# One filter spectrum of a block convolution by a direct transform instead of two stages with shuffles, on one core of Trainium2

## The chip, the cores and the metric

The kernel runs on one core of a Trainium2 chip, as one launch. The metric is the device time of one execution in microseconds (us), the median of several runs. The engines are TensorE (PE, with its weight loads PEld), VectorE (DVE), ScalarE (ACT), GpSimd (POOL) and SyncE (SP), which here only issues DMAs. Every engine runs its own instructions in the order in which the program has them, so an instruction that waits holds up all that stand behind it on its engine.

## What is computed

The reference, cut to what matters (S = 2048 tokens, D = 640 columns, F = 1728, bf16):

```
x  = A_q
q  = layernorm(x)
ks = sum over t<4 of k shifted by t tokens * shift_k          # four taps
kv = ks * v
y  = irfft(rfft(kv, padded to 2S) * rfft(ssm_k, padded to 2S))[:S] + kv * ssm_D
h  = x + q * y                                                # a causal convolution along S, per column
n  = layernorm(h)
out = h + (silu(n @ w_gate) * (n @ w_up)) @ w_down            # the FFN
```

## The kernel before, in words

The tokens are cut into four blocks j = 0 to 3 of 512, the columns into two halves c = 0, 1 of 320. For each block and half the kernel computes a spectrum X of kv and a spectrum K of the filter ssm_k (1024 points, the block padded with as many zeros), multiplies spectra of blocks whose indices add up to j, and transforms back. The convolution of a block is followed by its layernorm and its FFN. A token 4p+b of a block lies in partition p, at place b.

**Two ways to a spectrum.** Block 0 goes the dense way (`dense_c`, L692): for each of four groups h of frequencies, `dense_h` (L678) multiplies the four slices b by 128x128 tables for the real and the imaginary part. These are 8 matmuls of 320 columns (op `df`), accumulated in PSUM and moved to SBUF by one instruction of 640 columns (`de`). Blocks 1 to 3 go in two stages (`conv_c`, L1086). `fwd` (L648) multiplies each slice b by two tables (op `s1`, 2 matmuls of 128x128 by 320 columns), moves the result to SBUF (`e1`, 640 columns) and then, by four DMAs from SBUF to SBUF of 160 KB (`sh`, one for each group, each needing all four `e1`), brings every fourth partition together. `spec` (L730) multiplies a shuffled group by a small table (op `s2`, 4 matmuls of 128x64 tables by 320 columns, pairs of which run beside each other on the two halves of the array) and moves the spectrum to SBUF (`e2`). The way back has the same two stages (`i2`, `e3`, shuffles `rs`, `i1`); in block 0 it is dense (`di`).

A name such as `s1K10b2` is read: first stage, filter K (or values X), block 1, column half 0, slice b2. `s2K10h1` is the second stage of group h1. The name of `G` in `shK10G1` is the group. Further ops in what follows: `kvn`, `kva`, `kvv` (DVE: taps, products and sums that make kv), `tap` (moves the taps from PSUM to SBUF), `m1`, `m2`, `cr`, `ci`, `ac` (DVE: products and sums of spectra), `kf` (DVE: the filter spectrum of a block put together with that of the block before), `w` and `h` (ACT and DVE: the convolution's result, scaled and added to x), `bn`, `ag`, `va`, `nr`, `nm` (layernorm statistics; `nr` is a power on POOL), `hn` (the normalised row, on ACT or DVE), `tr` (10 transposes on PE; L1119), `te` (their move to SBUF on ACT), `gu` (FFN, gate or up), `si` (silu, ACT), `gm` (gate times up, DVE), `dn` (FFN, down), `l0s`, `l0v` (sums for the first layernorm, ACT).

**Data.** Filters of blocks 1 to 3 come from DRAM by a transposing DMA (`kraw`, L597) and four copies of 80 KB (`shk`), which bring them into the layout of 4p+b; a first stage or a dense transform needs all four. The inputs k, v and x come as `kin`, `vin` and `x`; `kin` and `vin` of blocks after the first share one buffer each, so that a load waits until the one before has been used. The dense tables `den` (8 DMAs of 256 KB; ("f",h) forward, ("i",h) back) lie where w_down (`wd`) is put later, so `load_weights` (L1130) lets `wd` wait for the last op that reads a dense table (`den_last`). The tables of the two stages (`tab`, 640 KB, L1261) come in one DMA: 256 columns of first stage, 256 of last stage back (s1i), 1024 of second stage (w2s) and 1024 of its inverse (w2i) (a column is 2 bytes in each of 128 partitions, so 256 bytes).

**Warm-up.** `warm` (WARM = 5 and 4 matmuls of 512 columns) and five `fill` ops (2 such matmuls each) compute nothing that is used; they stand in PE's order like other work.

**The order.** It is not found at run time. `_PLAN` (L1288) is a packed table that gives every op its engine, its place in that engine's order, its buffer, and for some DMAs one more op to wait for (written `a<b`: a is issued when b is done). `plan` (L101) reads it, `emit` (L151) writes the instructions and the semaphore waits. All matmuls are recorded under the helper's line L515, evacuations under L495 (ACT) and L496 (DVE), DVE two-operand ops under L737, DMA issues under L503.

Of the kernel before, what the change touches and what calls it, by code (L numbers as in the profile page):

```python
# [255 lines left out]
def _tables(R, neg=False):  # L256
# [27 lines left out]
    cols = [s1f.reshape(128, -1), s1i.reshape(128, -1), w2s, w2i.reshape(128, -1)]  # L284
# [33 lines left out]
def bass_sequential_preLN__ssm_conv_h3__swiglu_ffn__prompt_kernel(  # L318
# [21 lines left out]
    FILL = [2, 2, 2, 2, 2]  # L340
# [6 lines left out]
    ACCD = 2560  # L347
    KDMA = [[False, False], [True, True], [True, True], [True, True]]
# [5 lines left out]
    tab_np, (oS1, oS1I, oW2, oW2I, *more_) = _tables(R, PEC)  # L354
# [8 lines left out]
    with ExitStack() as es:  # L363
# [208 lines left out]
        def load_kv(j, c, prio):  # L572
# [12 lines left out]
            if j == 0:  # L585
                dma([(lambda: V2(kt, 3 * CW, CW, 4, CW), lambda: dram(K2, c * CW, [[R * D, 128], [D, 4], [1, CW]]))], 328, [], [(kt, 0)], prio,
                    name=f"kin{j}{c}o", eng=LE)
            else:
                dma([rows(0, 128)], 573, [], [(kt, 0)], prio, name=f"kin{j}{c}", eng=LE)
# [100 lines left out]
        nks = {}  # L690

        def dense_c(c):  # L692
# [10 lines left out]
            for h in range(R):  # L703
# [17 lines left out]
        den_last = [None]  # L721
# [8 lines left out]
        def spec(nm, r, u, h, dst, off, prio):  # L730
            pt = Pair("p2")
# [64 lines left out]
        def inv2(j, c, ht_, parts, prio):  # L796
# [12 lines left out]
            pe(all_, CW, len(all_) // 2, rd + [(TAB, 1)], [(pt, "*") for pt in pts], prio, reserve=[(ht_[h], 0) for h, _, _ in parts],  # L809
# [28 lines left out]
        def agm(l, j):  # L838
            o = oAG + j * 8
# [6 lines left out]
        def ln_stats(l, j, b, c, xt, prio):  # L846
            vec(dve1(CW, False), lambda v: v.bn_stats(st6(l, j, b, c), V(xt, b * D + c * CW, CW)), [(xt, (b, c))],  # L847
                [(ST, ("s", l, j, b, c))], prio, name=f"bn{l}{j}{b}{c}")

        def ln_aggr(l, j, b, prio):  # L850
            vec(0.16, lambda v: v.bn_aggr(ag(l, j, b), st6b(l, j, b)), [(ST, ("s", l, j, b, c)) for c in range(2)],
# [34 lines left out]
        def ln_act(l, j, prio):  # L886

            xt = xts[j]
            for b in range(4):
# [37 lines left out]
        def kv_block(j, c, prio):  # L927
# [10 lines left out]
            tm = [P.tile(f"t{j}{c}{i}", "PP") for i in range(3 if j else 4)]  # L938
            t0 = tm[0]

            def mul2(jj, a_, b_):
# [4 lines left out]
                def both():  # L946
# [3 lines left out]
                k0, st = ((3 - jj) * CW, -CW) if j else (3 * CW, 0)  # L950
                vec(dve2(2 * W4), tt(both, lambda: cyc(kt, k0, st), lambda: cyc(TAPS, jj * D + c * CW, D), ALU.mult),
                    [(kt, 0), (TAPS, (c, jj // 2))], [(a_, 0), (b_, 0)], prio, name=f"kvn{j}{c}")
# [5 lines left out]
            if j == 0:  # L958
# [101 lines left out]
        def conv_bp(j, c, bp, HTt, pr, ready=None):  # L1060
# [8 lines left out]
            if not ready:  # L1069
                pe(fns, CW, 4, [(HTt, h) for h in range(R)] + [(TAB, 0)], [(pt, "*")], pr, name=f"i1{j}{c}{bp}")  # L1070
# [15 lines left out]
        def conv_c(j, c):  # L1086
# [3 lines left out]
            uk = fwd(f"K{j}{c}", [(kts[j, c], oS1)], pb + 104)  # L1090
            ux = fwd(f"X{j}{c}", [(vins[j, c], oS1)], pb + 101)
# [38 lines left out]
        def load_weights():  # L1130
# [20 lines left out]
            piece([(lambda: V(WD, 13 * D, D, 0, 64), lambda: dram(B_w_down, 13 * 128 * D, [[D, 64], [1, D]]))], 82, [(WD, 13)], "wdl", [den_last[0]])  # L1151
# [93 lines left out]
        def block_j(j):  # L1245
# [5 lines left out]
            if j == 0:  # L1251
# [9 lines left out]
                dma([(lambda: tab[:, :], lambda: tab_dram.ap())], 900, [], [(TAB, 0), (TAB, 1)], 90, name="tab")  # L1261
# [116 lines left out]
```

## Time and profile before

| | us |
|---|---|
| median of 3 runs | 283.43 (282.67 to 283.63) |
| the profiled execution | 282.72 |
| its span, first to last instruction | 280.8 |
| PE busy in it | 270.0 |
| DVE busy | 229.0 |
| ACT busy | 198.2 |

The span is read from the profile, the execution's own time stands 1.9 us above it and 0.71 us below the median. Busy time of PE is that of instructions as modelled: a matmul counts from its start to its end, and matmuls overlap, so a busy PE can be slower than its peak. A row of the timeline is a run of like instructions: its start, its length, the engine, line, operation, shapes and count, and in brackets the idle time before it with what ended that.

### The profile page before, as it was taken

The page shows a single profiled execution, that of the slowest core. Times are in us where ns is not written, and L with a number is a line of the kernel's source. Part 1 is how long each engine was busy: PE and PEld are TensorE (multiplying, and loading weights), DVE is VectorE, ACT ScalarE, POOL GpSimd, SP SyncE. Part 2 cuts the span into 40 slices and gives each one's busy share as a digit, 9 for nine tenths or more (in the row PEclk, how much of TensorE's full clock was granted, in tenths as well). Part 3 has the DMA queues.
Part 4 walks back from the last instruction along what each step waited for, and adds up shares of the span by engine and source line. Part 5 has one row for each costly group of instructions (what it writes and reads, how often), then busy time and mean ns, then how long its engine had stood idle before and what let it go on. Part 6 is the DMA issues. An engine that isn't in the chain of part 4 may idle for free.

```text
span 280.8 us, 4821 instructions
## 1 busy us (share of the span) xinstructions
PE 270.0 (96%) x1735; PEld 149.8 (53%) x1735; DVE 229.0 (82%) x423; ACT 198.2 (71%) x322; POOL 13.9 (5%) x21
## 2 busy tenths in 40 slices
PE   8999996789999999999999999999999999999996
PEld 3667663355544467644344666544445675444574
DVE  3989999699999999999989999999997742224133
ACT  4648888799999979777899979769998830321100
POOL 1000100100000202000000103000002010000000
PEclk9999999799999999999999999999999999999999
DMA  6978979968986780685533364660012043000012
GB/s 189 267 234 259 213 234 247 261 167 249 307 262 208 231 260 7 167 229 177 175 103 98 97 232 137 168 237 1 0 70 99 21 77 89 0 2 0 0 37 82
DMA packets 54461, 41.37 MB, mean 147 GB/s; under 512 B 20195, under 2 KB 51748, under 8 KB 54438
## 3 DMA queue, kind: packets, MB, share of 16 engines
q1 hardware_dynamic: 54290, 41.02, 49.9%
q8 instruction: 14, 0.23, 0.3%
q14 instruction: 9, 0.07, 0.1%
q10 hardware_dynamic: 148, 0.04, 0.1%
HBM read 19.42 MB, written 2.62 MB: 78 GB/s over the span
## 4 chain that ended last, share of the span: by engine, by line
PE 63%; DVE 16%; DMA 8%; ACT 6%; SPq 4%; issue 2%; POOL 0%; ACTq 0%
PE ps L515 63%; DVE sb L737 15%; DMA sb<-in_A_k_dram 4%; SPq L503 3%; ACT sb L495 3%; DMA sb<-sb 3%; DMA sb<-cst_den 1%; ACT sb L1074 1%; SPq L597 1%; ACT sb L1173 1%; ACT L1173 0%; POOL stt L864 0%; DVE sb L1240 0%; ACT sb L879 0%; ACT sb L891 0%
## 5 line engine op out<-in xcount | busy, mean ns | idle before, releaser
L515 PE MATMUL ps<-sb 128*128 128x320 bf16 (+2 forms) x1259 | 226.8, 335 | 2.5 <-DVE sb L529 1.1
L737 DVE TENSOR_TENSOR sb<-sb 128x1280 bf16<-128x1280 bf16 (+5 forms) x264 | 174.3, 732 | 5.4 <-ACT sb L495 3.0
L515 PEld LDWEIGHTS ps<-sb 128*128 128x128 bf16 (+1 forms) x1259 | 120.3, 98 | 95.0 <-issue 7.8
L495 ACT ACTIVATE sb<-ps 128x640 bf16<-128x640 f32 (+2 forms) x161 | 113.3, 755 | 24.5 <-PE ps L515 18.4
L515 PE MATMUL ps<-sb,tab 128*64 128x320 bf16 (+2 forms) x432 | 53.0, 308 | 4.2 <-DMA sb<-sb 3.2
L1173 ACT ACTIVATE sb<-ps 128x1024 bf16<-128x1024 f32 (+2 forms) x32 | 29.1, 920 | 33.3 <-PE ps L515 33.2
L515 PEld LDWEIGHTS ps<-sb,tab 128*64 128x64 f16 (+2 forms) x432 | 26.2, 103 | 29.5 <-issue 10.3
L737 DVE TENSOR_TENSOR sb<-ps,sb 128x1024 bf16<-128x1024 f32 (+3 forms) x18 | 16.0, 893 | 26.2 <-PE ps L515 19.6
L864 POOL TENSOR_TENSOR stt<-stt 128x2 f32<-128x2 f32 (+1 forms) x12 | 12.9, 1080 | 213.7 <-DVE stt L863 183.8
L1074 ACT ACTIVATE sb<-ps,stt 128x320 f32<-128x320 f32 x32 | 17.8, 621 | 2.7 <-PE ps L515 2.3
L1078 DVE SCALAR_TENSOR_TENSOR sb<-sb,stt 128x320 bf16<-128x320 bf16 x32 | 16.7, 548 | 1.4 <-ACT sb L1074 1.4
L1240 DVE SCALAR_TENSOR_TENSOR sb<-ps,stt,sb 128x640 bf16<-128x640 f32 x12 | 10.6, 881 | 3.5 <-PE ps L515 3.4
L898 ACT ACTIVATE sb<-sb,stt 128x640 uint8<-128x640 bf16 x16 | 13.3, 831 | 0.1
L891 ACT ACTIVATE sb<-sb 128x640 uint8<-128x640 bf16 x16 | 11.9, 742 | 0.4 <-DMA sb<-in_A_q_dram 0.4
L916 ACT ACTIVATE sb<-sb,stt 128x640 uint8<-128x640 bf16 x12 | 9.9, 829 | 1.3 <-DVE stt L911 0.9
L1215 DVE SCALAR_TENSOR_TENSOR sb<-ps,stt,sb 128x320 bf16<-128x320 f32 x8 | 4.4, 551 | 6.7 <-PE ps L515 6.7
L879 ACT ACTIVATE sb<-sb,stt 128x640 bf16<-128x640 bf16 x7 | 6.4, 915 | 0.4 <-DVE stt L871 0.2
L878 DVE TENSOR_SCALAR sb<-sb,stt 128x640 bf16<-128x640 bf16 x9 | 3.9, 444 | 0.7 <-PE ps L1119 0.6
L847 DVE BATCH_NORM_STATS2 stt<-sb 128x6 f32<-128x320 bf16 x8 | 3.5, 482 | 0.0
L635 PE MATMUL ps<-sb 128*128 128x128 bf16 (+1 forms) x24 | 3.2, 225 | 0.1
L891 ACT ACTIVATION_READ_ACCUMULATOR sb<-sb 128x1 f32 x16 | 3.3, 204 | 0.0
L898 ACT ACTIVATION_READ_ACCUMULATOR sb<-sb,stt 128x1 f32 x16 | 3.2, 201 | 0.0
(26 smaller groups left out, 21.6 us busy)
## 6 DMA issues: line engine op xcount, KB each, us to landing
sb<-sb SPq DMA_DIRECT2D x72, 160.0 KB, 2.4
sb<-in_A_k_dram SPq DMA_DIRECT2D x6, 560.0 KB, 4.6
sb<-in_A_v_dram SPq DMA_DIRECT2D x8, 320.0 KB, 4.1
sb<-in_A_q_dram SPq DMA_DIRECT2D x8, 320.0 KB, 3.4
sb<-cst_den SPq DMA_DIRECT2D x8, 256.0 KB, 3.7
sb<-sb SPq DMA_DIRECT2D x24, 80.0 KB, 3.3
out_dram<-sb SPq DMA_DIRECT2D x12, 160.0 KB, 2.1
sb<-in_B_w_down_dram SPq DMA_DIRECT2D x3, 480.0 KB, 5.1
```

The lines of the kernel that those rows point to most:

```text
L495: fns = {"act": lambda a: a.activation(out=dst(), in_=src(), func=ACTF.Copy), "dve": lambda v: v.tensor_copy(out=dst(), in_=src())}
L503: fns = [(lambda g, d=d, s=s: g.dma_start(d(), s())) for d, s in subs]
L515: return lambda t: t.matmul(o(), l(), r(), start=st, stop=sp)
L737: return lambda v: v.tensor_tensor(out=o(), in0=a(), in1=b_(), op=op)
L864: P.op({"pool": 1.05}, lambda g: g.tensor_tensor(out=y, in0=va, in1=stt[:, oCO + 4:oCO + 4 + hi - lo], op=ALU.pow), c1 + [(ST, "half")], c ...
L891: P.op({"act": act_c(D) + 0.22}, lambda a, b=b, jt=jt: a.activation(out=JU(jt), in_=V(xt, b * D, D), func=ACTF.Copy, accum_out=tmv(l, j, 4 ...
L898: P.op({"act": act_c(D) + 0.3}, lambda a, b=b, jt=jt: a.activation(out=JU(jt), in_=V(xt, b * D, D), func=ACTF.Square, bias=tmv(l, j, 5)[:, ...
L916: P.op({"act": act_c(D) + 0.3}, lambda a, b=b, jt=jt: a.activation(out=JU(jt), in_=V(xt, b * D, D), func=ACTF.Square, bias=tmv(l, j, 5)[:, ...
L1074: P.op({"act": act_c(CW, True)}, lambda a, k=k, b=b, wt=wt: a.activation(out=VF(wt, CW), in_=B32(pt, k, CW), func=ACTF.Identity, scale=tmv ...
L1078: vec(dve1(CW), lambda v, b=b, wt=wt, xv=xv: v.scalar_tensor_tensor(out=xv(), in0=xv(), scalar=tmv(0, j, 5)[:, b:b + 1], in1=VF(wt, CW), o ...
L1173: P.op({"act": act_c(n)}, lambda a: a.activation(out=dst(), in_=src(), func=ACTF.Silu), rd, wr, -1000, name=f"si{j}{i}")
L1240: vec(dve1(640), lambda v: v.scalar_tensor_tensor(out=hv(), in0=B32x2(pt, CW), scalar=tmv(0, j, 5)[:, b:b + 1], in1=hv(), op0=ALU.subtract ...
```

## The change

Three things change. The filters of block 1, column half 0, are transformed by the dense tables; the table DMA is cut in three; and the packed table of orders is another one.

```diff
-    cols = [s1f.reshape(128, -1), s1i.reshape(128, -1), w2s, w2i.reshape(128, -1)]
+    cols = [s1f.reshape(128, -1), w2s, s1i.reshape(128, -1), w2i.reshape(128, -1)]
...
+    DFW = {("K",1,0)}
...
-        def dense_h(nm, src, h, dst, prio, neg=None):
+        def dense_h(nm, src, h, dst, prio, neg=None, off=None):
+            off = h * 640 if off is None else off
...
-            pe(fns, CW, len(fns), [(src, 0), (src, 1), (DEN, ("f", h))], [(pt, "*")], prio, reserve=[(dst, h)], name=f"df{nm}h{h}")
-            evac(lambda: V2(dst, h * 640, CW, 2, CW), lambda: B32x2(pt, CW), 2 * CW, [(pt, "*")], [(dst, h)], prio, name=f"de{nm}h{h}")
+            df = pe(fns, CW, len(fns), [(src, i) for i in range(4)] + [(DEN, ("f", h))], [(pt, "*")], prio, reserve=[(dst, h)], name=f"df{nm}h{h}")
+            evac(lambda: V2(dst, off, CW, 2, CW), lambda: B32x2(pt, CW), 2 * CW, [(pt, "*")], [(dst, h)], prio, name=f"de{nm}h{h}")
...
-                den_last[0] = last
+                dens.append(last)
...
         def spec(nm, r, u, h, dst, off, prio):
+            if not isinstance(u, list):
+                dense_h(r + nm, u, h, dst, prio, off=off)
+                return
...
-            uk = fwd(f"K{j}{c}", [(kts[j, c], oS1)], pb + 104)
-            ux = fwd(f"X{j}{c}", [(vins[j, c], oS1)], pb + 101)
+            dk, dx = ((y, j, c) in DFW for y in "KX")
+            uk = kts[j, c] if dk else fwd(f"K{j}{c}", [(kts[j, c], oS1)], pb + 104)
+            ux = vins[j, c] if dx else fwd(f"X{j}{c}", [(vins[j, c], oS1)], pb + 101)
...
-                      [(WD, f) for f in range(a_, b_)], "wd", [den_last[0]])
+                      [(WD, f) for f in range(a_, b_)], "wd", dens)
...
-                dma([(lambda: tab[:, :], lambda: tab_dram.ap())], 900, [], [(TAB, 0), (TAB, 1)], 90, name="tab")
+                for i_, (lo, hi) in enumerate(((0, oW2), (oW2, oS1I), (oS1I, tab_np.shape[1]))):
+                    dma([(lambda lo=lo, hi=hi: tab[:, lo:hi], lambda lo=lo, hi=hi: tab_dram.ap()[:, lo:hi])], 0.256 * (hi - lo), [], [(TAB, i_)],
+                        90 + 10 * i_, name=f"tab{i_}")
```

So four `s1`, four `e1`, four `sh` and four `s2` of K10 go; four `df10K` of 8 matmuls and four `de10K` come. `wd` waits for every reader of a dense table, `df10K` among them. The pieces of the table are 64 KB (first stage), 256 KB (second stage) and 320 KB (both of the way back), each waited for by its own readers. The diff holds further switches that are set to what the kernel did before (`KVP`, `L0D`), and moves of statistics that only they would use.

The orders that the two packed tables hold, written out around the change. PE, from the first inverse op of half 1 of block 0 on:

```
before: di1h0 s1K10b1 s1K10b2 di1h1 s1K10b0 s1X11b2 di1h2 s1X11b1 s1X11b3 di1h3 s1X11b0 s2X10h2 s2K10h1 fill
        s2K10h3 s2K10h0 s2K10h2 s2X10h3 s1K11b0 s1K11b3 fill fill s1K11b2 s2X10h0 tr00 tr01 s1K11b1 gu000
after:  di1h0 s1X11b3 s1X11b1 di1h1 df10Kh0 s1X11b2 di1h2 s1X11b0 di1h3 df10Kh1 df10Kh2 s1K11b1 fill s1K11b0
        df10Kh3 s2X10h1 s2X10h3 s2X10h2 s1K11b2 fill warm s1K11b3 s2X10h0 tr00 s2X11h2 tr01 gu001
```

In the order before, `s1K10b3` stands ahead of `di1h0`, and a `warm` of 4 matmuls stands early, behind the first transposes `ktr00`; in the order after this `warm` is the one seen above, and one `fill` stands behind the first `warm`. DVE, from the last statistics of block 0 on, and ACT around the same place:

```
DVE before: va10 l1m0 va10 kf102 kf102 nm10 kf100 hn01 m1a102 nm10 kf100 hn03 hn02 kva20
DVE after:  va10 l1m0 va10 kva20 kf100 nm10 kva20 hn01 nm10 kf102 kf102 hn03 hn02 kvv20
ACT before: e1X11b0 e2X10h2 e2K10h1 e2K10h3 e2K10h2 e2K10h0 e1K11b3 e1K11b0 hn00 e1K11b2 e2X10h3 te00 te01
ACT after:  de10Kh1 e1K11b1 e1K11b0 de10Kh2 de10Kh3 e2X10h3 e2X10h1 e1K11b2 hn00 e1K11b3 e2X10h2 te00 te01
```

`tap00` and `tap11` are on DVE in the order after (before: `tap01` alone), the others on ACT. SP, from the table DMA on:

```
before: tab den(i,2)<vin10 kraw10<vin01 den(i,3) kin20 shk10 shk10 vin11 shk10 shk10 wu00 wg03<shk10
        shX10G3 shX10G1 shX10G0 shX10G2 kraw11<wu00 wu03 wg13 shK10G1 shK10G3 shK10G2 shK10G0
        shk11 shk11 shk11 shk11 kin21 shX11G0 wg00
after:  tab0 den(i,0) vin10 den(i,1) den(i,3) kraw10<vin01 kin20 x11 shk10 shk10 wu00<den(i,3) vin11 shk10 shk10
        kraw11<wu00 shX10G0 wg03<shk10 tab1<shk10 wg13 shX10G2 shk11 shk11 shk11 shX10G3 shk11 shX10G1
        wu23 shX11G0 shX11G3 shX11G2 wg00 vin20 kin21<shX11G2 wu03
```

At the start of SP's order `kin10` stands ahead of den(f,1) and behind `x00` in the order after (before: behind den(f,1)), den(f,2) and den(f,3) stand behind `x01`, ahead of any ("i",h). The third piece `tab2` stands far back, behind the pieces of the FFN's weights. The orders further on, for all engines, are other ones too, with the same ops in them.

More of the change, by code (lines that the diff above doesn't have):

```diff
@@ L838, in agm @@
         def agm(l, j):
[L839 removed]
+            o = (oAG if l else oTM + 12) + j * 8
             return stt[:, o:o + 8].rearrange("p (b s) -> p b s", b=4)[:, :, 0:1].rearrange("p b s -> p (b s)")
@@ L847, in ln_stats @@
             vec(dve1(CW, False), lambda v: v.bn_stats(st6(l, j, b, c), V(xt, b * D + c * CW, CW)), [(xt, (b, c))],
-                [(ST, ("s", l, j, b, c))], prio, name=f"bn{l}{j}{b}{c}")
+                [(ST, ("s", 1, j if l else 1, b, c))], prio, name=f"bn{l}{j}{b}{c}")
         def ln_aggr(l, j, b, prio):
-            vec(0.16, lambda v: v.bn_aggr(ag(l, j, b), st6b(l, j, b)), [(ST, ("s", l, j, b, c)) for c in range(2)],
+            vec(0.16, lambda v: v.bn_aggr(ag(l, j, b), st6b(l, j, b)), [(ST, ("s", 1, j if l else 1, b, c)) for c in range(2)],
                 [(ST, ("a", l, j, b))], prio, name=f"ag{l}{j}{b}")
@@ L888, in ln_act @@
             xt = xts[j]
+            if j == 0 and L0D:
+                for b in range(4):
+                    for c in range(2):
+                        ln_stats(0, j, b, c, xt, prio)
+                    ln_aggr(0, j, b, prio)
+                vec(0.16, lambda v: v.tensor_scalar(out=tmv(l, j, 5), in0=agm(l, j), scalar1=-1.0, scalar2=None, op0=ALU.mult),
+                    [(ST, ("a", l, j, b)) for b in range(4)], [(ST, ("negm", l, j, b)) for b in range(4)], prio, name=f"l{l}m{j}")
+                ln_rstd(l, j, prio, False, range(4))
+                return
             for b in range(4):
@@ L936, in v4 @@
                 return V2(t, off, CW, 4, CW)
-            tm = [P.tile(f"t{j}{c}{i}", "PP") for i in range(3 if j else 4)]
+            tm = [P.tile(f"t{j}{c}{i}", "PP") for i in range(4 if j == 0 and KVP[c] else 3)]
             t0 = tm[0]
@@ L956, in add2 @@
                     [(t0, 0), (b_, 0)], [(t0, 0)], prio, name=f"kva{j}{c}")
-            if j == 0:
+            if j == 0 and KVP[c]:
                 mul2(0, tm[0], tm[1])
@@ L1069, in conv_bp @@
             if not ready:
-                pe(fns, CW, 4, [(HTt, h) for h in range(R)] + [(TAB, 0)], [(pt, "*")], pr, name=f"i1{j}{c}{bp}")
+                pe(fns, CW, 4, [(HTt, h) for h in range(R)] + [(TAB, 2)], [(pt, "*")], pr, name=f"i1{j}{c}{bp}")
             for k in range(2):
```

150 lines of the change are left out of this document (79 added, 71 removed).

## The prediction

> **What bounds the kernel now.** The page's first rows say that PE is busy nearly throughout.
>
> ```profile
> PE 270.0 (96%) x1735; PEld 149.8 (53%) x1735; DVE 229.0 (82%) x423; ACT 198.2 (71%) x322; POOL 13.9 (5%) x21
> ```
>
> The mean hides one stage, so the next view is busy time by stretches of 5 us (columns: the stretch, then PE, PEld, DVE, ACT, POOL busy, granted clock, DMA share, GB/s), and two stretches asked for by themselves.
>
> ```profile
> 45.00:50.00 5.00, 1.98 (x15) 0.56 (x14) 5.00 (x17) 4.72 (x9) 0.00 (x0) 0.96 0.88 263
> 50.00:55.00 5.00, 4.60 (x26) 2.09 (x26) 3.20 (x13) 3.27 (x5) 1.36 (x2) 0.70 0.98 287
> 55.00:60.00 5.00, 4.19 (x44) 3.26 (x45) 4.43 (x7) 5.00 (x9) 0.00 (x0) 1.00 0.91 218
> 60.00:65.00 5.00, 4.18 (x28) 1.75 (x26) 5.00 (x8) 4.86 (x7) 0.00 (x0) 1.00 0.56 163
> ...
> 49.62:53.03 3.41, 3.03 (x17) 1.56 (x18) 1.61 (x12) 1.62 (x3) 1.36 (x2) 0.50 0.97 238
> 65.00:278.00 213.00, 211.97 (x1337) 114.27 (x1335) 171.40 (x313) 149.08 (x243) 10.38 (x9) 1.00 0.41 123
> ```
>
> From 65 us on PE stands idle for 213.00 - 211.97 = 1.0 us in all. What PE does not get done before 65 comes out at the end, one for one; what it gets done earlier comes off. Between 45 and 65 it is idle for 3.02 + 0.40 + 0.81 + 0.82 = 5.05 us and has half its clock for 3.41 us. That is the stage to read. PE's timeline there:
>
> ```profile
> 43.60 1.25 PE L515 MATMUL ps<-sb 128*128 128x320 bf16 x8
> 44.69 1.02 PE L515 MATMUL ps<-sb,tab 128*128 128x320 bf16 x6
> 47.81 0.46 PE L515 MATMUL ps<-sb,tab 128*64 128x320 bf16 x4 [2.10 <-DMA sb<-sb]
> 50.00 2.99 PE L515 MATMUL ps<-sb,tab 128*64 128x320 bf16 x16 [0.80 <-DMA sb<-sb]
> 55.19 0.73 PE L1119 MATMUL ps<-sb 128*128 128x128 bf16 x10 [0.59 <-ACT sb L879]
> 56.54 0.73 PE L1119 MATMUL ps<-sb 128*128 128x128 bf16 x10 [0.61 <-DVE sb L878]
> 57.51 4.55 PE L515 MATMUL ps<-sb 128*128 128x256 bf16 x30
> 62.88 1.25 PE L515 MATMUL ps<-sb 128*128 128x512 bf16 x5 [0.82 <-ACT sb L1173]
> 64.06 1.01 PE L515 MATMUL ps<-sb,tab 128*64 128x320 bf16 x12
> 65.00 1.25 PE L515 MATMUL ps<-sb 128*128 128x512 bf16 x5
> ```
>
> By the written order the matmuls at 47.81 are `s2K10h1`, those at 50.00 begin with `s2K10h0` and `s2K10h2`. The two waits of 2.10 and 0.80 us are for shuffles of K10. The SP timeline and the chain that ended last show why they are late: eight DMAs issued one behind the other, and the copy on the chain lands 4.6 us after the fourth.
>
> ```profile
> 23.16 0.61 SPq L503 DMA_DIRECT2D tab<-cst_tab x1
> 26.38 1.82 SPq L597 DMA_TRANSPOSE sb<-in_A_ssm_k_dram  x1
> 40.19 2.12 SPq L597 DMA_TRANSPOSE sb<-in_A_ssm_k_dram  x1
> 43.48 5.13 SPq L503 DMA_DIRECT2D sb<-sb  x8
> ...
> 45.35 4.61 DMA sb<-sb
> ...
> sb<-sb SPq DMA_DIRECT2D x4, 80.0 KB, 3.5
> sb<-in_A_ssm_k_dram SPq DMA_TRANSPOSE x1, 4.9
> ```
>
> The last two rows are issues in the window 36 to 50, with us to landing. DVE, POOL and ACT show the other thing that is late there, the layernorm that must come before the FFN:
>
> ```profile
> 50.13 0.16 DVE L863 TENSOR_SCALAR stt<-stt 128x2 f32<-128x2 f32 x1
> 52.06 1.02 DVE L737 TENSOR_TENSOR sb<-sb 128x640 bf16<-128x640 bf16 x2 [1.77 <-ACT sb L495]
> 52.99 0.15 DVE L871 TENSOR_TENSOR stt<-stt 128x2 f32<-128x2 f32 x1
> 53.46 0.44 DVE L878 TENSOR_SCALAR sb<-sb,stt 128x640 bf16<-128x640 bf16 x1
> 56.03 0.45 DVE L878 TENSOR_SCALAR sb<-sb,stt 128x640 bf16<-128x640 bf16 x1 [0.57 <-PE ps L1119]
> 56.40 0.82 DVE L737 TENSOR_TENSOR sb<-sb 128x1280 bf16<-128x1280 bf16 x1
> ...
> 50.23 1.36 POOL L864 TENSOR_TENSOR stt<-stt 128x2 f32<-128x2 f32 x2 [15.84 <-DVE stt L923]
> ...
> 40.27 1.30 ACT L495 ACTIVATE sb<-ps 128x640 bf16<-128x640 f32 x2 [0.65 <-PE ps L515]
> 54.22 0.92 ACT L879 ACTIVATE sb<-sb,stt 128x640 bf16<-128x640 bf16 x1
> ```
>
> POOL has both powers ready at 50.23 + 1.36 = 51.59, but the `nm` that takes them runs at 52.99: two `kf` stand ahead of it in DVE's order and wait for the evacuation of K10's groups h2 and h3. So the shuffles of K10 hold up the layernorm of block 0 as well, and through it the transposes at 55.19 and 56.54 and the first FFN matmuls at 57.51.
>
> **The change part by part.** *PE's work.* Eight matmuls of 320 columns take 44.69 - 43.60 = 1.09 us, 0.136 each; twelve with 64-column tables take 65.00 - 64.06 = 0.94 us, 0.078 each. K10 loses 8 x 0.136 + 16 x 0.078 = 2.34 us and gains 32 x 0.136 = 4.36 us: PE has 2.0 us more to do. With all else the same and no gap closed, that is what the change costs.
>
> *Where it lies.* Ahead of `tr00`, PE had 2.34 us of K10; now it has 4.36 us, and `s1K11b1` (0.27) and `s2X10h1` (0.31) besides, 2.6 us more. After `tr00` it therefore has 2.6 - 2.0 = 0.6 us less. The result is the shift of that point less 0.6 us.
>
> *When PE can be at `tr00`.* `di1h3` ended its issue at 44.69 before; `df10Kh0` (1.09) replaces the first stage of K10 (1.09), and `s1X11b0` (0.27) comes ahead, so 44.96. Then two dense groups 2.18, `s1K11b1` 0.27, a fill 0.43 (two matmuls of 512 columns; five take 64.06 - 62.88 = 1.18 us at most), `s1K11b0` 0.27, the last dense group 1.09, three `s2X10` 0.94, `s1K11b2` 0.27, fill and warm 1.28, `s1K11b3` 0.27, `s2X10h0` 0.31: 7.31 us, so 52.3. No DMA of K10 is left in this list; its cover is the four groups of dense work.
>
> *When the rows are normalised.* The statistics end at 50.13 as now. The DVE work ahead of them is the same but for one tap evacuation more, against an earlier issue of `kin10`, for which DVE now stands:
>
> ```profile
> 4.52 0.82 DVE L496 CAST sb<-ps 128x640 bf16<-128x640 f32 x1 [2.39 <-PE ps L515]
> 15.33 2.35 DVE L737 TENSOR_TENSOR sb<-sb 128x2560 bf16<-128x2560 bf16 x2 [1.04 <-DMA sb<-in_A_k_dram]
> ```
>
> The bounds are +0.8 and -1.0 us; the two lie near each other, and I take nothing. Then a `kva` (0.8, as at 56.40), a `kf` (0.4), `nm` at 51.4 instead of 52.99, a `kva`, the first `hn` to 52.6, `nm`, two `kf`, two more `hn` to 54.2. The `kf` ahead of `nm` needs groups h0 and h1, whose dense matmuls end by 47. On ACT four evacuations at 1.30 / 2 = 0.65 us go, and `hn00` follows `e1K11b2`, 51.3 to 52.2. So `tr00` runs at 52.6, `tr01` at 54.2, and the first FFN matmul at 54.9 in place of 57.51: 2.6 us earlier. DVE no longer stands for 1.77 us, so it is ahead by as much.
>
> *The DMAs.* SP issues four shuffles less (4 x 5.13 / 8 = 2.6 us of SP, 640 KB). Who needs the table and when, and the first `wd`:
>
> ```profile
> 30.35 0.71 PE L515 MATMUL ps<-sb,tab 128*128 128x320 bf16 x4
> 82.59 0.99 PE L515 MATMUL ps<-sb,tab 64*128 64x320 bf16 x12
> ...
> 68.70 0.54 SPq L503 DMA_DIRECT2D sb<-in_B_w_down_dram  x1
> ```
>
> The pieces of the table: the first (64 KB) is needed at 30, the third at 82, the second (256 KB) by `s2X10` at 49; it is issued near 40, and its cover is some 5 us; were that gone, PE would wait one for one. `wd` now waits for `df10Kh3` at 49 instead of `di1h3` at 45; it is issued at 68 now, so the cover is 19 us: nothing.
>
> *The new wait.* `s1K11b1` stands ahead of the last dense group, all `s2X10` and `tr00`, and needs all four `shk11` by 47.1. The last X10 shuffle is behind the last `shk11` on SP. These follow the transposing load `kraw11`, which waits for `wu00` and for the first copies. Before, it was issued at 40.19 and the four copies by 43.48 + 5.13 = 48.61, landing at about 52.1 (3.5 us). Now `kraw10` need not wait behind `vin10`'s landing, as den(i,2) and with it `kraw10` did at 26.38, and the four K10 shuffles are gone from in front. I work it out at: `kraw11` between 35 and 40, landing 4.9 later, six issues of 0.64 behind it, landing 3.5 later: 47 to 52. PE would wait between nothing and 4.9 us. I take 1.2 us, near the early end, since nothing in the order keeps `kraw11` as late as 40.
>
> *Sum.* -2.6 - 0.6 + 1.2 = **-2.0 us**: 282.72 - 2.0 = 280.7 for an execution like the profiled one. The median of the runs stood 0.71 above it, so 281.4.
>
> The row 49.62:53.03 shows the clock at 0.50 for 3.41 us after PE's gap. The Trainium skill (TensorE: Matmul & The Clock Gate, Part 1) says that the clock is halved after at least one idle window of about 3.4 us, and that the window runs freely. The trace agrees in the length. By that rule a wait of 1.2 us keeps the clock whole, a long one brings the half clock back; the sum above goes without it.
>
> **The rivals.** *The chain before the FFN does not move.* If the normalised rows come when they did, because the statistics (DVE busy 5.00 of 5.00 up to 50) come later by what I count as gained, the point stays and only the 0.6 us count: 282.8 by the median. For it: DVE has no idle time there to give. Against: 1.77 us of DVE's idle time lie behind the statistics, and the two `kf` go from there.
>
> *The `shk11` copies are as late as before* (slower). Place: PE's order at `s1K11b1`. If they land at 52.1, the 5.1 us of the list from `s1K11b1` to `tr00` (7.31 less the two dense groups ahead, 2.18) put `tr00` at 57.2, 2.0 us later than 55.19; less 0.6, that is +1.4, and with a gap of 5 us the half clock of 3.41 us costs up to 1.7 more: +1.4 to +3.1, so 285.7 by its middle. It decides from a landing at 50.7 on (55.19 + 0.6 - 5.1). For it: the DMAs are at 0.88 to 0.98 of their share there, and `wu00` must land first. Against: the queue ahead is shorter by the four shuffles.
>
> *All of it closes*: no wait at the copies, -3.2 us, and with the 0.82 us at 62.88 gone too -4.0: 279.4 to 280.2.
>
> *The extra matmuls lie where PE has no gap*, the change doing nothing else: +2.0, so 285.4. The list above puts three of four dense groups in the gap from 45 on, so I count it within the slower case.
>
> The orders after 65 us are new as well. Since PE loses 1.0 us there now, they can give 1.0 at most; a bad one can take as much or more, of which this trace shows nothing. I allow 1 us to either side of each case.
>
> **How the numbers follow.** Forecast (-2.0, give or take 0.9) 0.48; all closes 0.14; the chain does not move 0.18; slower by the copies or the added matmuls 0.20. A measurement of this kernel can tell about 0.3% (0.85 us) from no change. Faster by over that: nearly all of the first, all of the second, a little of the third, 0.64. Within: most of the third and the edges, 0.18. Slower: 0.18. The range reaches from the case that all closes (279.4 to 280.2) past the unmoved chain with its 1 us (283.8) to just short of the slower case without loss of clock (283.43 + 1.4 = 284.8), most of which is left out: 279.5 to 284.4.
>
> **What would show it.** Right: no wait for a DMA longer than 1.5 us on PE between 45 and 56; the clock at 1.00 throughout the 50s; the first 10 transposes near 53, the first 256-column matmuls near 55; PE from 65 on as full as now. Wrong: a wait of several us before a first-stage pair near 48 (the copies); `nm` still at 53 (the chain); or the early shift in place and PE idle after 65, which would mean that the new orders further on lose it again.

## The result and the profile after

| | before | after |
|---|---|---|
| median, us | 283.05 (281.09 to 283.63, 4 runs) | 279.08 (278.76 to 281.23, 4 runs) |
| ratio | | 0.9889, 95% interval 0.9840 to 0.9939 |
| profiled execution, us | 282.72 | 278.87 |
| its span, us | 280.8 | 277.0 |
| first FFN matmul of block 0 | 57.51 | 54.65 |
| start of the last row of the chain | 278.07 | 274.27 |

The kernel became faster by 1.1%, 3.1 us by the ratio (1.7 to 4.5), 3.8 us between the two profiled executions. The forecast was 2.0 us, with a case at 3.2 to 4.0 that was called "all of it closes". By the ratio the kernel after takes, from the first median of before, 283.43 x 0.9889 = 280.3 us, inside the forecast range of 279.5 to 284.4; the median of its four executions, 279.08, lies 0.4 us below that range.

Beside the experiments the kernel before was executed 97 more times: the median is 282.1 us (280.4 to 284.2), 3.0 above the median of the kernel after. Executions in a slower state are in no ratio and no mean: one of the kernel before (284.76 us) and one of before_pe_load (978.61 us).

Busy time by stretches of the kernel after (columns as in the prediction: the stretch, then PE, PEld, DVE, ACT, POOL, granted clock, DMA share, GB/s):

```profile
45.00:50.00 5.00, 4.97 (x41) 2.98 (x39) 5.00 (x18) 5.00 (x10) 0.60 (x1) 1.00 0.93 278
50.00:55.00 5.00, 4.47 (x42) 2.43 (x41) 4.89 (x12) 5.00 (x8) 1.42 (x2) 1.00 0.89 267
55.00:60.00 5.00, 4.97 (x37) 2.86 (x35) 5.00 (x8) 4.97 (x7) 0.00 (x0) 1.00 0.74 183
60.00:65.00 5.00, 4.88 (x36) 2.05 (x37) 5.00 (x7) 5.00 (x9) 0.00 (x0) 1.00 0.85 236
65.00:274.00 209.00, 207.66 (x1304) 112.66 (x1301) 168.62 (x310) 144.53 (x237) 9.56 (x9) 1.00 0.40 120
```

Between 45 and 65 us PE's idle time went from 5.05 us to 0.03 + 0.53 + 0.03 + 0.12 = 0.71, and its clock is whole. From 65 on it idles 1.34 us (1.03 before): nothing of the gain was given back there. PE's timeline of the kernel after says how the gap went:

```profile
47.53 1.25 PE L518 MATMUL ps<-sb 128*128 128x320 bf16 x8
48.71 1.48 PE L518 MATMUL ps<-sb,tab 128*64 128x320 bf16 x14
50.34 1.47 PE L518 MATMUL ps<-sb 128*128 128x512 bf16 x6
51.65 0.83 PE L518 MATMUL ps<-sb,tab 128*128 128x320 bf16 x6
52.41 0.73 PE L1142 MATMUL ps<-sb 128*128 128x128 bf16 x10
53.69 0.73 PE L1142 MATMUL ps<-sb 128*128 128x128 bf16 x10 [0.16 <-DVE sb L891]
54.65 1.26 PE L518 MATMUL ps<-sb 128*128 128x256 bf16 x10 [0.23 <-ACT sb L498]
...
60.65 1.25 PE L518 MATMUL ps<-sb 128*128 128x512 bf16 x5
```

The row at 47.53 is the last dense group of K10, at 48.71 follows the second stage of X10, then fill and warm, and `tr00` at 52.41. No row waits for a DMA. The row at 60.65 is the first FFN row of 512 columns, which in the kernel before had 0.82 us of idle time ahead of it (62.88): that gap is closed too, with other matmuls in its place. DVE, POOL, ACT and SP of the kernel after:

```profile
49.30 0.16 DVE L876 TENSOR_SCALAR stt<-stt 128x2 f32<-128x2 f32 x1
50.79 0.16 DVE L884 TENSOR_TENSOR stt<-stt 128x2 f32<-128x2 f32 x1
51.60 0.44 DVE L891 TENSOR_SCALAR sb<-sb,stt 128x640 bf16<-128x640 bf16 x1
52.83 0.80 DVE L891 TENSOR_SCALAR sb<-sb,stt 128x640 bf16<-128x640 bf16 x2
...
49.40 2.01 POOL L877 TENSOR_TENSOR stt<-stt 128x2 f32<-128x2 f32 x2 [18.07 <-DVE stt L945]
...
51.28 1.00 ACT L892 ACTIVATE sb<-sb,stt 128x640 bf16<-128x640 bf16 x1
...
36.08 1.40 SPq L607 DMA_TRANSPOSE sb<-in_A_ssm_k_dram  x1
...
63.62 0.47 SPq L506 DMA_DIRECT2D sb<-in_B_w_down_dram  x1
```

The statistics end 0.83 us earlier (49.30 for 50.13), `nm` 2.20 earlier (50.79 for 52.99), the first normalised row 1.86 earlier. `kraw11` is issued at 36.08 instead of 40.19.

### The profile page after: what moved, and what is told of

Same layout as the page of the kernel before. It is cut to its first block, busy times and chain, and to the rows that moved or that the text cites. A ratio compares the mean times of both kernels' runs of the same rounds, so it can differ in the third digit from the quotient of the medians.

```text
span 277.0 us, 4814 instructions
## 1 busy us (share of the span) xinstructions
PE 270.9 (98%) x1743; PEld 151.4 (55%) x1743; DVE 229.5 (83%) x424; ACT 194.2 (70%) x317; POOL 13.6 (5%) x21
## 4 chain that ended last, share of the span: by engine, by line
PE 68%; DVE 12%; DMA 8%; ACT 5%; SPq 4%; issue 1%; ACTq 0%
PE ps L518 67%; DVE sb L750 12%; DMA sb<-sb 6%; ACT sb L498 4%; SPq L506 4%; DMA sb<-cst_den 2%; PE ps L645 1%; ACT sb L1096 1%; SPq L607 0%; ACT sb L892 0%; DVE sb L1238 0%; DVE sb L532 0%; DVE stt L916 0%; SPq L227 0%; ACTq L227 0%
## 5 line engine op out<-in xcount | busy, mean ns | idle before, releaser
L518 PE MATMUL ps<-sb 128*128 128x320 bf16 (+2 forms) x1291 | 232.5, 334 | 2.0 <-DVE sb L532 1.1
L518 PEld LDWEIGHTS ps<-sb 128*128 128x128 bf16 (+1 forms) x1291 | 123.6, 98 | 95.8 <-issue 6.5
L750 DVE TENSOR_TENSOR sb<-sb 128x1280 bf16<-128x1280 bf16 (+4 forms) x264 | 174.2, 730 | 1.7 <-ACT sb L498 0.6
L498 ACT ACTIVATE sb<-ps 128x640 bf16<-128x640 f32 (+2 forms) x156 | 109.8, 761 | 24.4 <-PE ps L518 18.4
L518 PE MATMUL ps<-sb,tab 128*64 128x320 bf16 (+2 forms) x408 | 50.5, 302 | 1.2 <-DMA sb<-sb 0.5
L518 PEld LDWEIGHTS ps<-sb,tab 128*64 128x64 f16 (+2 forms) x408 | 24.4, 101 | 24.6 <-issue 9.7
L1096 ACT ACTIVATE sb<-ps,stt 128x320 f32<-128x320 f32 x32 | 17.9, 619 | 4.6 <-PE ps L518 4.6
L499 DVE CAST sb<-ps 128x640 bf16<-128x640 f32 x2 | 1.6, 815 | 2.9 <-PE ps L518 2.9
```

The lines of the kernel that those rows point to most:

```text
L498: fns = {"act": lambda a: a.activation(out=dst(), in_=src(), func=ACTF.Copy), "dve": lambda v: v.tensor_copy(out=dst(), in_=src())}
L518: return lambda t: t.matmul(o(), l(), r(), start=st, stop=sp)
L750: return lambda v: v.tensor_tensor(out=o(), in0=a(), in1=b_(), op=op)
L1096: P.op({"act": act_c(CW, True)}, lambda a, k=k, b=b, wt=wt: a.activation(out=VF(wt, CW), in_=B32(pt, k, CW), func=ACTF.Identity, scale=tmv ...
```

## The experiments

The theory to be tested is the prediction's: PE's queue sets the end, what closes its gap ahead of the FFN comes off, one for one. After the first round a second theory stood against it: DVE's chain of products sets the end, and only its idle time counts. Twelve runs were made, one of them of the kernel before unchanged. For reading them two moments were taken from each profiled execution: the start of the first FFN matmul (the first row of 256 columns on PE) and the start of the last row of the chain. The difference is what the rest of the program takes. Each row is one execution; the ratio is that of all executions of the kernel.

| kernel | first FFN matmul | last row | rest | ratio to before (95%) |
|---|---|---|---|---|
| before | 57.51 | 278.07 | 220.56 | |
| before_again | 56.55 | 277.83 | 221.28 | |
| before_norm_first | 55.50 | 277.27 | 221.77 | 1.0044 (1.0019 to 1.0069) |
| before_warm_gap | 55.86 | 276.11 | 220.25 | 0.9995 (0.9972 to 1.0018) |
| before_dve_fill | 55.88 | 277.49 | 221.61 | 1.0004 (0.9980 to 1.0028) |
| before_dve_fill2 | 56.86 | 278.13 | 221.27 | 0.9991 (0.9965 to 1.0018) |
| before_dve_load | 57.18 | 277.93 | 220.75 | 0.9989 (0.9961 to 1.0017) |
| before_pe_load | 55.18 | 278.45 | 223.27 | 1.0066 (1.0033 to 1.0100) |
| dense_old | 57.79 | 279.51 | 221.72 | 1.0058 (1.0030 to 1.0086) |
| dense_keep | 56.73 | 277.09 | 220.36 | 1.0015 (0.9983 to 1.0048) |
| dense_dve_fill | 56.84 | 278.09 | 221.25 | 1.0036 (1.0012 to 1.0060) |
| dense_dve_fill2 | 57.12 | 277.91 | 220.79 | 1.0060 (1.0028 to 1.0092) |
| after | 54.65 | 274.27 | 219.62 | 0.9889 (0.9840 to 0.9939) |
| after_dve_gap | 54.19 | 279.57 | 225.38 | 0.9990 (0.9966 to 1.0014) |

**dense_old**: the dense K10 alone, in the orders before, with the table in one DMA.

```diff
+    DFW = {("K",1,0)}
 orders: s2K10h* -> dfK10h*, e2K10h* -> deK10h* in their old places; s1K10, e1K10, shK10 out
```

> The dense transform of K10 alone, in the orders before: the four first stages, their evacuations and the four shuffles are taken out of the orders, each second stage is replaced in its place by its dense group; table in one DMA as before. Theory (the wait for K10's shuffles was the gap): no PE wait for a DMA between 44 and 49, clock 1.00 throughout, first transposes near 52.6 in place of 55.19, and since K10 is complete ahead of them in both kernels nothing else changes: -2.3 us, a ratio near 0.992 to the kernel before. Rival (the new orders brought the gain, the dense form itself only costs its matmuls): 0 to +2.0 us, a ratio of 1.000 to 1.007.

Measured 283.24 us beside 281.98: slower by 0.6%, as the rival had it (0 to +2.0 us). PE's timeline of dense_old:

```profile
47.09 4.94 PE L518 MATMUL ps<-sb 128*128 128x320 bf16 x34 [1.07 <-ACT sb L1096]
51.96 1.31 PE L518 MATMUL ps<-sb,tab 128*64 128x320 bf16 x8
55.47 0.73 PE L1142 MATMUL ps<-sb 128*128 128x128 bf16 x10 [0.35 <-ACT sb L892]
57.79 4.55 PE L518 MATMUL ps<-sb 128*128 128x256 bf16 x29
```

The waits for the shuffles are gone, but all 32 dense matmuls stand in one run behind a wait of 1.07 us for a PSUM buffer that ACT empties (the convolution's result, L1096), where the small second stage stood. K10's spectrum is ready at 52, as with two stages. The dense form by itself brings its 2.0 us of PE work and nothing earlier.

**dense_keep**: as dense_old, with the first stage, evacuations and shuffles of K10 still run; their result is not used.

```diff
-            uk = kts[j, c] if dk else fwd(f"K{j}{c}", [(kts[j, c], oS1)], pb + 104)
+            uk = fwd(f"K{j}{c}", [(kts[j, c], oS1)], pb + 104)
+            uk = kts[j, c] if dk else uk
```

> As dense_old, but the first stage of K10, its four evacuations on ACT and its four shuffles on SP still run; nothing reads what they bring. PE has 1.09 us and ACT 2.6 us more than in dense_old, and SP and the DMAs carry the shuffles. Theory (what counted was that PE and the layernorm waited for the shuffles, not the work on ACT or in the queue): most of the gain stays, -1.2 to -1.9 us, ratio 0.993 to 0.996. Rival (relief of ACT and of the DMA queue is what pays): no gain, ratio 1.000 or more, with the transposes at 54 or later.

Measured 282.45 us, ratio 1.0015 with 1 inside. The number fits the rival (1.000 or more, transposes at 54 or later; `tr00` is at 54.42), but not its reason: dense_old has the relief of ACT and of the queue and is no faster. dense_keep does more work than dense_old and came out faster; the two intervals just overlap. Why is open.

**before_norm_first**: two stages, the layernorm's steps of block 0 ahead of `kf` on DVE, `hn00` two evacuations earlier on ACT.

```diff
-DVE: va10 kf102 kf102 nm10 kf100 hn01 m1a102 nm10 kf100 hn03 hn02 kva20
+DVE: va10 nm10 nm10 hn01 kf102 kf102 hn03 hn02 kf100 m1a102 kf100 kva20
-ACT: e2K10h0 e1K11b3 e1K11b0 hn00 e1K11b2
+ACT: e2K10h0 hn00 e1K11b3 e1K11b0 e1K11b2
```

> The kernel before, with the two nm and hn01 ahead of the two kf on DVE, hn03 and hn02 right behind those, and hn00 two evacuations earlier on ACT. Theory: the rows are normalised 1.0 to 1.6 us earlier, but PE's gap at 45 to 50 and its half clock stay and its list ahead of the transposes ends near 54.6, so they move by 0.6 at most: -0.6 to 0 us, ratio 0.998 to 1.000. Rival (the layernorm held up by kf was the whole of it): -1.6 us or more, ratio 0.994 or less.

Measured 1.0044, slower, which neither theory had. PE's timeline of before_norm_first:

```profile
52.68 0.46 PE L515 MATMUL ps<-sb,tab 128*64 128x320 bf16 x4 [0.75 <-ACT sb L495]
53.19 0.73 PE L1119 MATMUL ps<-sb 128*128 128x128 bf16 x10
55.50 4.55 PE L515 MATMUL ps<-sb 128*128 128x256 bf16 x29
...
64.83 0.44 PE L515 MATMUL ps<-sb,tab 128*128 128x320 bf16 x2 [0.58 <-DVE sb L737]
```

The transposes no longer wait, but PE now waits 0.75 us for an evacuation that `hn00` was put ahead of, and 0.58 us for a product that the layernorm was put ahead of. The gap moved. Why the whole is slower than before these rows do not show.

**before_warm_gap**: the filler ahead of `s2K10h1` instead of behind it, 10 matmuls instead of 2.

```diff
-    FILL = [2, 2, 2, 2, 2]      PE: s2X10h2 s2K10h1 fill s2K10h3
+    FILL = [2, 10, 2, 2, 2]     PE: s2X10h2 fill s2K10h1 s2K10h3
```

> The kernel before, with the fill behind s2K10h1 put ahead of it and made 10 matmuls of 512 columns, so that PE works through most of its wait of 2.10 us. Theory: the clock stays at 1.00 from 49 to 53, but the transposes wait for the normalised rows at 55.19 in any case, so -0.4 to +0.2 us, ratio 0.9985 to 1.0005. Rival (the half clock of 3.41 us was a loss of its own): -1.2 to -1.7 us, ratio 0.994 to 0.996.

Measured 0.9995, as the theory had it. PE's timeline of before_warm_gap:

```profile
46.19 2.33 PE L515 MATMUL ps<-sb 128*128 128x512 bf16 x10 [0.47 <-ACT sb L1074]
48.45 2.90 PE L515 MATMUL ps<-sb,tab 128*64 128x320 bf16 x24
55.86 4.55 PE L515 MATMUL ps<-sb 128*128 128x256 bf16 x29
```

The filler keeps the clock at 0.999 or above in all ten executions. The profiled execution was the quickest of the ten (280.68 us); the ten together are no faster than before.

**before_again**: the kernel before once more, with a profile only.

> The kernel before, unchanged, for a trace from the same chip as the other runs of this call. Both theories: the span between 279 and 281 us; the DVE instruction that ends the chain's DVE part near 213 to 214.5, and 64.2 us from there to the end of the span.

```profile
47.18 0.46 PE L515 MATMUL ps<-sb,tab 128*64 128x320 bf16 x4 [1.67 <-DMA sb<-sb]
49.19 2.85 PE L515 MATMUL ps<-sb,tab 128*64 128x320 bf16 x16 [0.52 <-DMA sb<-sb]
56.55 4.55 PE L515 MATMUL ps<-sb 128*128 128x256 bf16 x29
```

This is PE of before_again. The same program reaches the FFN 0.96 us earlier than in the first profile, and ends 0.24 us earlier.

**before_dve_fill** and **before_dve_fill2**: two stages; the sums `kva20` (the expectations call them products) go into DVE's waits for POOL, the rows ahead of `kf`; in the second kernel `hn02` stands behind `kf`.

```diff
-DVE: va10 kf102 kf102 nm10 kf100 hn01 m1a102 nm10 kf100 hn03 hn02 kva20 m2a102 kvn21 kva20
+DVE: va10 kva20 nm10 hn01 kva20 nm10 hn03 hn02 kf102 kf102 kf100 kf100 m1a102 m2a102 kvn21   (fill)
+DVE: va10 kva20 nm10 hn01 kva20 nm10 hn03 kf102 kf102 kf100 kf100 hn02 m1a102 m2a102 kvn21   (fill2)
 ACT of both: hn00 as in before_norm_first
```

> The kernel before with its two-stage K10; only the DVE order around block 0's layernorm is changed: the two kva20 that stood behind are put into the waits for the two powers, and the four kf behind the normalised rows; hn00 two evacuations earlier on ACT. Theory now (DVE is the engine that sets the end: the DVE part ends when its work and its idle time are through, and a fixed 64.2 us of PE follow): DVE's idle time of 2.3 us between 50 and 57 falls to 0.5 or less and the time with it, -1.5 to -2.0 us, ratio 0.993 to 0.995. Rival (PE's gap at 45 to 50 must close as well, since PE and DVE are both full to 214): -0.5 us or less, ratio 0.998 or more.

> The kernel before, two stages of K10 and all, with VectorE's queue between 50 and 57 us ordered so that the two products of kva20 stand in its waits for GpSimd, the rows hn01 and hn03 ahead of kf, and hn02 behind kf. If VectorE's idle time is what counts: its idle time in 50 to 57 falls from 1.6 us (before_again) to about 0.2, and the end comes 1.2 to 1.6 us earlier, ratio 0.994 to 0.996. If it does not count, or if the idle time comes back behind it: ratio 0.998 or above.

Measured 1.0004 and 0.9991. DVE of before_dve_fill, then PE of before_dve_fill2:

```profile
54.41 0.45 DVE L878 TENSOR_SCALAR sb<-sb,stt 128x640 bf16<-128x640 bf16 x1 [1.27 <-PE ps L1119]
```

```profile
53.36 0.46 PE L515 MATMUL ps<-sb,tab 128*64 128x320 bf16 x4 [1.40 <-ACT sb L495]
53.86 0.73 PE L1119 MATMUL ps<-sb 128*128 128x128 bf16 x10
55.45 1.08 PE L1119 MATMUL ps<-sb 128*128 128x128 bf16 x10 [0.86 <-DVE sb L878]
56.86 6.67 PE L515 MATMUL ps<-sb 128*128 128x256 bf16 x34
```

In the first, `hn02` waits 1.27 us for the buffer that PE's transposes read; the idle time is only moved. In the second, DVE's idle time in 50 to 57 fell from 1.61 us (before_again) to 0.67, but 0.85 us came up in 57 to 65 (none before), and PE got two new waits, 1.40 and 0.86 us. In neither kernel did the idle time go away, so they do not part the two theories; with two stages of K10 it came back elsewhere.

**dense_dve_fill** and **dense_dve_fill2**: the same two orders on dense_old.

> dense_old with the same DVE and ACT order as in before_dve_fill, so the dense transform and the DVE order together, all else as before. Theory (DVE alone): as before_dve_fill or up to 1.3 us worse, as dense_old stood 1.3 us above the kernel before; ratio 0.993 to 0.999. Rival (both gaps must close): clearly better than before_dve_fill, -2.0 to -3.0 us, ratio 0.989 to 0.993.

> Dense K10 in the orders of the kernel before (which alone measured 1.0058), with the same VectorE order as before_dve_fill2. If VectorE's idle time is what counts: idle in 50 to 57 falls from 2.3 us to about 0.3, ratio 1.0058 less 0.006 to 0.008, that is 0.998 to 1.000. If the dense form itself is what costs: ratio 1.004 or above. If the dense spectrum is what pays once VectorE is free: 0.992 or below.

Measured 1.0036 and 1.0060: no better than dense_old. The first lies outside what either theory gave, the second is where it was put if the dense form itself costs. Nor did the filling work as it was meant to: between 50 and 57 DVE idles 3.07 us in the first and 1.46 in the second (2.33 in dense_old; about 0.3 had been expected of the second). So these two do not test a DVE without idle time. PE of dense_dve_fill2:

```profile
46.48 4.94 PE L518 MATMUL ps<-sb 128*128 128x320 bf16 x34 [1.07 <-ACT sb L1096]
54.80 0.73 PE L1142 MATMUL ps<-sb 128*128 128x128 bf16 x10
```

`hn01` ran at 51.52 there, yet `tr00` starts at 54.80 with no idle time before it: PE is still working off what stands ahead. In this kernel, with the dense form in the old order, PE's list sets when the FFN begins, not the layernorm.

**after_dve_gap**: the kernel after, with `kva20` and `kf102` taken out of the waits and put behind the rows.

```diff
-DVE: va10 kva20 kf100 nm10 kva20 hn01 nm10 kf102 kf102 hn03 hn02 kvv20
+DVE: va10 kf100 nm10 nm10 hn01 hn03 hn02 kf102 kf102 kva20 kva20 kvv20
```

> The changed kernel with the two kva20 and the two kf102 moved behind the normalised rows on DVE, so that DVE stands while POOL works out the two powers: 1.5 us of idle time come back, while the rows are normalised 0.7 us earlier than in the changed kernel. Theory (DVE sets the end): 1.0 to 1.5 us above the changed kernel, ratio to the kernel before 0.993 to 0.995. Rival (the point at which PE can begin the FFN sets it): 0 to 0.7 us below the changed kernel, ratio 0.986 to 0.989.

Measured 0.9990 of before, 3.0 us above the kernel after by the medians: moving four instructions loses the whole gain. Both theories missed it; the one by which the start of the FFN sets the end had even the direction wrong. The FFN starts 0.46 us earlier than in the kernel after (54.19 for 54.65), and the loss comes behind it. DVE of after_dve_gap, then the last of these instructions in the kernel after:

```profile
50.00 0.16 DVE L884 TENSOR_TENSOR stt<-stt 128x2 f32<-128x2 f32 x1 [0.59 <-POOL stt L877]
52.79 0.45 DVE L891 TENSOR_SCALAR sb<-sb,stt 128x640 bf16<-128x640 bf16 x1 [1.26 <-PE ps L1142]
82.03 0.16 DVE L916 TENSOR_SCALAR stt<-stt 128x4 f32<-128x4 f32 x1
```

```profile
79.99 0.17 DVE L916 TENSOR_SCALAR stt<-stt 128x4 f32<-128x4 f32 x1
```

DVE idles 2.42 us between 45 and 57 (0.11 in the kernel after), and the same statistic, with the same work ahead of it, comes 2.04 us later. PE of after_dve_gap:

```profile
54.19 1.27 PE L518 MATMUL ps<-sb 128*128 128x256 bf16 x10 [0.16 <-ACT sb L498]
...
93.03 0.72 PE L518 MATMUL ps<-sb,tab 64*128 64x320 bf16 x8 [1.09 <-DVE sb L750]
...
136.91 0.45 PE L518 MATMUL ps<-sb,tab 64*128 64x320 bf16 x4 [1.12 <-ACT sb L1196]
138.13 0.45 PE L518 MATMUL ps<-sb,tab 64*128 64x320 bf16 x4 [0.77 <-ACT sb L498]
```

PE waits for DVE at 93.03 and for ACT at 137; between 65 and 140 it idles 1.93 + 2.84 = 4.77 us (1.08 in the kernel after). This profiled execution was the slowest of its twelve (284.13, the median 282.06) and the only one with less than a whole clock (0.993), so its 225.38 in the table overstates the loss by about 2, and the waits at 137 may be its own.

**before_pe_load**: ten more filler matmuls, ahead of the second stage of K30.

```diff
-    FILL = [2, 2, 2, 2, 2]
+    FILL = [2, 2, 12, 2, 2]
```

> The kernel before with ten more filler matmuls (0.215 us each, +2.1 us of TensorE work) in the filler that stands ahead of the second stage of K30, between 150 and 180 us, in a stretch where TensorE has almost no idle time. If TensorE's queue of work sets the end one for one, as the prediction took it: +2.1 us, ratio 1.0075 (1.005 to 1.010). If VectorE's chain of products sets the end and TensorE only follows it from about 214 us on: 0 to +0.5 us, ratio 1.000 to 1.002, and VectorE's end stays at about 214.

Measured 1.0066: +1.9 us (0.9 to 2.8) for 2.15 us of work. PE of before_pe_load:

```profile
46.89 0.46 PE L515 MATMUL ps<-sb,tab 128*64 128x320 bf16 x4 [1.14 <-DMA sb<-sb]
55.18 4.55 PE L515 MATMUL ps<-sb 128*128 128x256 bf16 x29
176.93 2.75 PE L515 MATMUL ps<-sb 128*128 128x512 bf16 x12
```

The load is in the last row. The rest takes 223.27 us, 221.12 without the load, as in the other kernels. DVE, which has no idle time from 180 to 214 in before_again, idles 1.32 us there, waiting for evacuations by ACT, which come after the delayed matmuls. Work put on PE where PE is full comes out at the end, nearly one for one, and the second theory in this form, DVE alone, which expected 0 to 0.5 us, falls. The test says nothing of an earlier start.

**before_dve_load**: a memset in 32 pieces on DVE behind `hn02`.

```diff
-vec(0.4, lambda v: v.memset(V(GUT, 13 * 512, 512, 64, 128), 0.0), ..., name="gz")
+vec(0.4, [lambda v, c=c: v.memset(V(GUT, 13 * 512 + c * 16, 16, 64, 128), 0.0) for c in range(32)], ..., name="gz")
 order: gz behind hn02
```

> The kernel before with the memset of the last gate chunk's padding cut into 32 pieces and moved to VectorE's queue behind hn02, at about 55.5 us: +2.1 to +4.7 us of VectorE work (0.075 to 0.155 us a piece, less the 0.27 us of the whole one), TensorE's work unchanged. If VectorE's chain sets the end: the end comes later by what the pieces take, less what of it falls into VectorE's later waits (about 2.4 us of idle time stand between 57 and 178): +1 to +4 us, ratio 1.004 to 1.015. If TensorE's queue sets the end: 0, ratio 0.998 to 1.002.

Measured 0.9989. DVE of before_dve_load shows why this tells nothing:

```profile
56.22 0.55 DVE L1150 MEMSET sb<- 64x8 uint32 x32
```

The 32 pieces took 0.55 us in all, 0.28 more than the one memset (0.27), not the 2.1 or more that the theories were given. How much free time DVE has there was not measured.

**Not tried**: the new orders with K10 in two stages, since they presuppose K10's buffers to be free. So how the gain divides between the dense form and the new orders is open: the dense form without them costs 0.6%, and what they would bring without it no run shows.

## Why the prediction was right, and where it was not

- *PE sets the end, one for one*: half right. before_pe_load shows it for added work. For the start of the FFN the table agrees where the orders further on are those of before: in these twelve executions the first FFN matmul lies anywhere from 55.18 to 57.79, the rest (before_pe_load less its 2.15) between 220.25 and 221.77. For a time this looked refuted: before_norm_first and before_warm_gap reached the FFN 1.7 to 2.0 us earlier than the first profile and were not faster. But the unchanged code reaches it at 57.51, 56.55 and 55.18 in three executions (before, before_again, and before_pe_load, which is the same up to there). The early FFN of the two kernels lies within that spread, so it cannot be put down to their edits; the comparison was with the latest of three. What does not hold is that an earlier start of PE comes off by itself. In after_dve_gap PE has all of it (0.68 us of idle time between 45 and 65, 0.72 in the kernel after) and the gain is gone; in its trace DVE is 2 us behind and PE then waits for it. Between 65 and 140 PE and DVE are both full in the kernel after (73.92 and 73.95 of 75 us), so the earlier start is kept only if both have it. The prediction says that DVE "is ahead by as much"; that sentence entered no term of its sum, and the gain hangs on it.
- *The shuffles make PE's gap, K10 holds up the layernorm*: right in the trace after (no DMA wait, `nm` 2.20 us earlier). But the dense form in the old orders (dense_old and its three variants) does not bring the FFN forward (56.73 to 57.79). The gain came with the new orders, in which the groups come before 48.8 and DVE's waits are filled: after_dve_gap undoes only the filling, and the whole gain goes.
- *2.0 us more PE work, 0.6 us less of it behind* `tr00`: the rest is 219.62 for 220.56 to 221.28 in the three traces of unchanged code (before_pe_load less its load), 0.9 to 1.7 us less. The gap at 62.88 (0.82) is gone as well. That and the 0.6 make 1.4; no run parts the two.
- *When PE and the rows are there*: `tr00` 52.6 predicted, 52.41 measured; `tr01` 54.2 and 53.69; the first FFN matmul 54.9 and 54.65. The statistics came 0.83 us earlier, inside the bounds (+0.8 to -1.0) of which nothing had been taken; POOL's two powers gave part of it back, 2.01 us in place of 1.36.
- *The DMAs*: the table's pieces cost nothing. The first `wd` is issued at 63.62 and nothing waits for it. The prediction and the section on the change are wrong on one point: `wd` does not wait for K10's dense groups, since the list of those readers is copied while block 0 is recorded, before K10's (`dfK10h0` to `h3` in the code) are in it. It changes no number.
- *The new wait at* `s1K11b1`: **this term failed**, mis-sized. `kraw11` was put between 35 and 40 and came at 36.08; the wait was put at 1.2 us, within 0 to 4.9, and is 0. PE went from `di1h3` to `tr00` with nothing but its own work (52.3 by the list, 52.41 measured). The right reading was in the same sentence: nothing in the order kept `kraw11` as late as 40, so the early end was the likelier one. By the prediction's own rows it was also priced too high: PE at 52.3 + 1.2 = 53.5 is 0.9 us behind the rows at 52.6, not 1.2.
- *The sum*: without that wait -3.2 us, measured -3.1 (1.7 to 4.5). With the gap at 62.88, -4.0; the profiled pair gives -3.8. That is the case "all of it closes", which was given 0.14. That the terms add up so well is in part luck. The 2.6 us were counted from the trace of before in which the FFN starts latest. The mean of the three traces of unchanged code is 56.41, with 220.99 for the rest; against it the FFN of the kernel after starts 1.76 us earlier and the rest is 1.37 shorter, 3.1 together. By this count the first term was too large and the 0.6 too small. The kernel after has one trace, so its own spread is not known.

## What to carry to other kernels

Before a profile is taken as the baseline of a stage, profile the unchanged kernel two or three times: here one and the same matmul started at 55.18, 56.55 and 57.51, a spread larger than most effects that were looked for, and an edit judged against the latest of them looks like a gain. The moment at which a stage starts and the time that the rest takes are better kept apart. Where two engines are both full behind a stage, a sum for one of them is not enough: here PE started as early as ever and the gain was lost, because the other engine had stood idle for 2.4 us. And the transform without shuffles, left in the old places, was 0.6% of added time.

## What the runs showed of the hardware that was not expected

**POOL beside DVE.** The two powers take 1.36 us in the kernel before, where DVE stands idle beside them, and 2.01 us in the kernel after, where it runs sums with two inputs (1280 columns the first). Putting those sums into DVE's wait lengthened the wait itself. POOL of before_dve_fill2, which has K10 in two stages and the same filling:

```profile
50.13 2.06 POOL L864 TENSOR_TENSOR stt<-stt 128x2 f32<-128x2 f32 x2 [16.14 <-DVE stt L923]
```

The Trainium skill (GPSIMD Engine Reference, 8. Key points) says that GpSimd shares its SBUF interfaces with VectorE and contends with instructions of two SBUF inputs; these sums have two, and the rows agree.

**The half clock.** In 53 of the 97 executions of the kernel before the granted clock was under 0.995, in 44 it was 0.999 or above; their means are 282.52 and 281.96 us, 0.6 us apart. That is at most its price, since longer waits on PE could bring both. All four executions of the kernel after had 1.000 and the ten of before_warm_gap 0.999 or above, and the mean of these ten (281.79) is near that of before with a whole clock: over all executions the clock is worth some 0.3 us, a tenth of the gain. It does not go by the length of the wait alone: PE waited 1.67 and 0.52 us in before_again and got half the clock (16 matmuls in 2.85 us), 1.67 and 0.67 us in before_dve_fill and kept it (16 in 1.98). A window that runs freely, as the Trainium skill has it (TensorE: Matmul & The Clock Gate, Part 1), would do that; no run here shows the window itself. Its other words, an idle window of about 3.4 us, do not fit: in the kernel before the longest wait ahead of the half clock was 2.10 us, with matmuls from 47.81 to 49.20 behind it.

**Small memsets.** 32 memsets of 8 words in a row took 17 ns each, though each is shown with 65 ns.
